# Sliding-window attention into a two-layer MLP: the order of the first loads and visits, and the form of the last output tile

## The chip, the core and the metric

The kernel runs on one core of a Trainium2 chip, in one launch. The metric is the device time of that core in microseconds (us); the time given for a kernel is the median of its runs. A core has TensorE (PE, matrix multiply, with its weight loads PEld), VectorE (DVE), ScalarE (ACT), GpSimd (POOL) and SyncE (SP). In this kernel POOL mostly issues DMAs that load and convert float32 to bfloat16, and SP issues the stores and the DMA transposes.

## The reference

Attention over 8 batches, 8 heads, 576 positions and head size 64, in which a position sees only those at most 32 away; its output, rearranged to 4608 tokens of 512, goes through a layer with an elementwise function between two matrix products.

```python
def _attn_ref(q, k, v) -> np.ndarray:
    B, H, S, D = q.shape
    window = 32
    scale = 1.0 / np.sqrt(D)
    scores = scale * np.matmul(q, k.transpose(0, 1, 3, 2))
    pos = np.arange(S)
    mask = np.abs(pos[:, None] - pos[None, :]) <= window
    scores = np.where(mask, scores, -1000000000.0)
    scores = scores - np.max(scores, axis=-1, keepdims=True)
    attn = np.exp(scores)
    attn = attn / (np.sum(attn, axis=-1, keepdims=True) + 1e-09)
    return np.matmul(attn, v).astype(np.float32)
...
def _moe_ref(x, w_in, w_out) -> np.ndarray:
    h = x @ w_in
    beta = 1.0
    neg = h <= -beta
    pos = h >= beta
    mid = ~neg & ~pos
    g = np.where(pos, h, np.where(neg, 0.0, (h + beta) ** 2 / (4.0 * beta)))
    _ = mid
    return (g @ w_out).astype(np.float32)
...
    x = np.ascontiguousarray(attn_out.transpose(0, 2, 1, 3)).reshape(B * S, H * D)
    return _moe_ref(x=x, **moe_kwargs)
```

Here x has 4608 rows of 512, w_in is 512 by 2048 and w_out 2048 by 512. The inputs are random; the output is float32.

## The kernel before

**Visits.** The second half of the problem sets the beat. The 4608 tokens are cut into 18 blocks of 256 (`TB`), the 2048 hidden columns into 8 groups of 256. The loop at L423 goes over visits a = 8 t + f: visit a multiplies the block t of x (kept transposed as `xT`, a ring of four batches' tokens) by the group f of w_in, eight matmuls of 256 columns into the PSUM tile `hp` (L444). ACT then computes `rr`, a rectified half of h + 1 (L448); DVE makes `mx`, the larger of h and `rr` (L450), and `gT`, the product of `rr` capped at 1 with `mx` (L451), which is the elementwise function. There are 144 visits and 8 turns of the loop without one.

**Quarters.** The second product runs in quarters. Quarter x (L405) is the quarter ff = x mod 4 of the hidden rows for the output tile tt = x div 4 of 128 tokens: four matmuls of 512 columns into the PSUM tile `op` (L414). After its fourth quarter a tile is copied to SBUF by ACT (L420) and stored by SP (L421). From visit 16 on, quarter a - 8 follows visit a; the first eight stand in a table (L364), as quarter needs the piece of `w_out` with its number ff and the `gT` of two visits. The last tile of all (`last`) is treated apart: it runs column quarter by column quarter, each with all 16 hidden groups (16 matmuls of 128 columns), a copy and a store of its own.

**Attention** is placed between the visits, by hand, in the table `ev` (L365 to L391): `scores` and `scores8` (L202, L229) multiply k by q and take the exponential on ACT; `sums` (L256) multiplies by v and by ones, and its end computes ln and exp on ACT (L290, L291) and leaves a DVE multiply into `xT` in the list `muls`, which `flush` (L302) issues later. `eng` tells how the band mask is put on: as matmuls on PE that add a bias ahead of the scores (`add_mask`, L195) when it is None, as a DVE multiply (L193) otherwise. The attention of batch b must be in `xT` before the blocks that hold its tokens are visited.

**Loads and transposes.** For the batches 0 to 2 (`LONG`), q and k come in two halves of four DMAs each (`load_long`, L80) and are transposed on PE (`tpose`, L169) through PSUM tiles of `ps_s` and `ps_n`, one buffer each, with a copy to SBUF by ACT or DVE; from batch 3 on SP's DMA transposes do it (`xpose`, L184). The lists of POOL's DMA issues are written out at L148 to L155 with `put` and `mix`; `load_w_in` (L104) loads a range of w_in's columns for one half h of the partitions, so a range needs two DMAs. POOL's issues run in their order; each one waits for the landing of the eighth before it, as eight semaphores are used in turn. `qjp` (L50) is a pool from which nothing is taken.

**The start.** Ahead of the loop (L328 to L356) the first half of batch 0 is transposed and goes through scores and sums, with matmuls on zeros in between (`keep_warm`, L314). The second half of batch 0 is transposed at visit 1 (L392: q at position 1, k at 1.5), its scores and sums are placed at visits 2 to 5 (L378 to L381), and visit 8 is the first that needs its tokens. PSUM: `ps_h` has two buffers for `hp`, `ps_o` two for `op` (visits 6 and 7 and `scores8` of batch 0 borrow them), `ps_s` and `ps_n` one pair of banks each.

Of the kernel before, what the change touches and what calls it, by code (L numbers as in the profile page):

```python
# [15 lines left out]
def kernel(  # L16
# [19 lines left out]
    nc = tc.nc  # L36
    B, H, S, D = q.shape
    NT, DM, DFF = out.shape[0], 512, 2048
# [3 lines left out]
    MAIN = 480  # L42
# [4 lines left out]

    const = ctx.enter_context(tc.tile_pool(name="const", bufs=1))
    nat = ctx.enter_context(tc.tile_pool(name="nat", bufs=2))
    qjp = ctx.enter_context(tc.tile_pool(name="qjp", bufs=2))  # L50
    ktp = ctx.enter_context(tc.tile_pool(name="ktp", bufs=3))
    ptp = ctx.enter_context(tc.tile_pool(name="ptp", bufs=2))
    smp = ctx.enter_context(tc.tile_pool(name="smp", bufs=2))
# [21 lines left out]
    V, P, A = nc.vector, nc.gpsimd, nc.scalar  # L75
# [65 lines left out]
    def halves(b, half):  # L141
        return [(load_long, b, half, t, y) for t in range(2) for y in range(NY)]

    def put(todo):
        for fn, *x in todo:
            fn(*x)

    w = [(load_w_in, c, c + d, h) for c, d in ((0, 256), (256, 256), (512, 512), (1024, 512), (1536, 512)) for h in range(2)]  # L148
    x = halves(0, 1)
    put(w[:4] + x[:4] + w[4:5] + x[4:] + w[5:])  # L150
    mix(halves(1, 0), [(load_w_out, 0)])
    put([(load_w_out, 1), (load_w_out, 2)] + [(load_v, 1, n) for n in range(4)])
    mix(halves(1, 1), [(load_w_out, 3)])
# [102 lines left out]
    def sums(b, y1, lo, hi, pool=ps_n):  # L256

        bb = two_banks(pool)
        w = hi - lo
        todo = []  # L260
        if lo < MAIN:
            ys, D0 = (y1,), w
            for par in range(2):
                a0 = max(lo, 32 * par)
                off = 32 - 64 * par
                todo.append((None, a0 - lo, hi - lo, lambda a, h, par=par, a0=a0, off=off: (
                    pt[b][HD[a], h, y1, par, a0 + off:hi + off])))
                for c2 in range(4):
                    q0, q1 = max(0, 128 * c2 - off, lo), min(128 * c2 + 128 - off, hi)
                    if q0 < q1:  # L270
                        todo.append((NC * y1 + 2 * c2 + par, q0 - lo, q1 - lo, lambda a, h, par=par, q0=q0, q1=q1, off=off: (
                            pt[b][HD[a], h, y1, par, q0 + off:q1 + off])))
        else:
            ys, D0 = (0, 1), 2 * w
            todo.append((None, 0, 2 * w, lambda a, h: pt8[b][HD[a], h].rearrange("p y j -> p (y j)")))
            for y in ys:
                todo.append((NC * y + 8, y * w, y * w + w, lambda a, h, y=y: pt8[b][HD[a], h, y]))
                for c in (None, NC * y + 7):
                    todo.append((c, y * w, y * w + 64, lambda a, h, y=y: pt[b][HD[a], h, y, 1, 448:512]))
        for n, (c, c0, c1, p) in enumerate(todo):  # L280
            o = D0 if c is None else 0
            for a in range(2):
                for h in range(2):
                    nc.tensor.matmul(bb[HD[h], a, o + c0:o + c1], ones[HD[a]] if c is None else vn[b][HD[a], c, h],  # L284
                                     p(a, h), start=n == 0, stop=True, skip_group_check=True)

        def end():
            lr = smp.tile([128, 2, 256], FP, name="lr", bufs=1)
            rc = smp.tile([128, 2, 256], FP, name="rc")
            A.activation(lr[:, :, :D0], bb[:, :, D0:2 * D0], AF.Ln)  # L290
            A.activation(rc[:, :, :D0], lr[:, :, :D0], AF.Exp, scale=-1.0)  # L291
            r0 = (b * S + lo) % RING
            o = xT.rearrange("p (a y) t -> p a y t", a=2)[:, :, ys[0]:ys[-1] + 1, r0:r0 + w]
            if len(ys) == 1:
                o = o[:, :, 0]
                muls.append(lambda: V.tensor_mul(o, bb[:, :, :D0], rc[:, :, :D0]))  # L296
            else:
                like = "p a (y j) -> p a y j"
                muls.append(lambda: V.tensor_mul(o, bb[:, :, :D0].rearrange(like, y=2), rc[:, :, :D0].rearrange(like, y=2)))  # L299
        return end  # L300

    def flush():  # L302
        while muls:
            muls.pop(0)()
# [56 lines left out]

    NB = NT // TB
    NF = DFF // 256
    quarters = {11: ([], [0]), 12: ([], [1]), 13: ([], [2]), 14: ([], [4, 5]), 15: ([6], [3, 7])}  # L364
    ev, tps = {}, {}  # L365

    def at(a, *todo):

        ev.setdefault(a, []).extend(x for x in todo if x)

    def steps(b, cut):

# [2 lines left out]
                yield (sums, b, y1, lo, hi), (scores, b, (y1, y1 + 1), (0, 2), (2 * k, 2 * k + 2))  # L375
        yield (sums, b, 0, MAIN, S), (scores8, b)

    at(2, (scores, 0, (0, 1), (0, 2), (2, 4)), (scores8, 0, ps_o))  # L378
    at(3, (sums, 0, 0, TB, MAIN), (scores, 0, (1, 2), (0, 2), (2, 4)))
    at(4, (sums, 0, 1, TB, MAIN, ps_s))  # L380
    at(5, (sums, 0, 0, MAIN, S))  # L381
    seq = [x for b in range(1, B) for x in steps(b, 224)]
    at(15, seq[0][0], (*seq[1][0], ps_s))
    for n, a in enumerate((20, 22, 23, 27)):
        at(a, seq[2 + n][0])
    for n, a in enumerate((11, 12, 19, 20, 22, 26, 27)):
        at(a, seq[n][1])
    sl = [30, 32, 35, 39, 42, 45, 49, 52, 56, 59, 62, 65, 69, 73, 77, 81, 84, 88, 92]
    sl += [96, 99, 103, 106, 110, 113, 116, 120, 124, 128]
    for n, a in enumerate(sl):  # L390
        at(a, seq[6 + n][0], seq[7 + n][1] if n < len(sl) - 1 else None)  # L391
    for b, half, *a in ((0, 1, 1, 1.5), (1, 0, 9, 10), (1, 1, 17, 18), (2, 0, 24, 25), (2, 1, 28, 29)):  # L392
        for t in range(2):
            tps[a[t]] = [(b, 2 * half + part, t) for part in range(2)]
    loads, xps = {}, {}
    for b in range(LONG, B):
        a = sl[5 * (b - 1) - 7] - 17
# [7 lines left out]
    def quarter(x):  # L405

        tt, ff = divmod(x, 4)
        if tt not in op:
            op[tt] = ps_o.tile([128, DM], FP, name="op", tag="op"), []
        o, done = op[tt]  # L410
        rows, last = slice(128 * tt, 128 * tt + 128), tt == NT // 128 - 1
        c = slice(128 * ff, 128 * ff + 128) if last else slice(0, DM)
        for j in range(2 * NF) if last else range(4 * ff, 4 * ff + 4):
            nc.tensor.matmul(o[:, c], gT[tt // 2][:, j, 128 * (tt % 2):128 * (tt % 2) + 128], w_out[:, j, c],  # L414
                             start=j == 0 if last else not done, stop=j == 2 * NF - 1 if last else len(done) == 2 * NF - 1,
                             skip_group_check=True)
            done.append(j)
        if last or len(done) == 2 * NF:
            osb = osp.tile([128, DM], FP, name="osb")
            A.copy(osb[:, c], o[:, c])  # L420
            nc.sync.dma_start(out=out[rows, c], in_=osb[:, c])  # L421

    for a in range(NF * NB + NF):  # L423
        t, f = divmod(a, NF)
        eng = None if a < 12 else V
        pre, post = quarters.get(a, ([], [a - NF] if a >= 2 * NF else []))
        for b, x in loads.get(a, []):
            if x < 2:
                load_nat(b, x)
            else:  # L430
                for n in range(4):
                    load_v(b, n)
        flush()
        if t < NB:
            if f == 0:
                gT[t] = gtp.tile([128, 2 * NF, TB], BF, name="gT", tag="gT")
            r0 = TB * t % RING
            if a in (6, 7):
                hp = ps_o.tile([128, 2, TB], FP, name="hp", tag="op")
            else:  # L440
                hp = ps_h.tile([128, 2, TB], FP, name="hp", tag="hp")
            for j in range(2):
                for n, kk in enumerate((0, 2, 1, 3)):
                    nc.tensor.matmul(hp[:, j], w_in[:, kk, 256 * f + 128 * j:256 * f + 128 * j + 128],  # L444
                                     xT[:, kk, r0:r0 + TB], start=n == 0, stop=n == 3)

            rr = ewp.tile([128, 2, TB], FP, name="rr")
            A.activation(rr, hp, AF.Relu, scale=0.5, bias=0.5)  # L448
            mx = ewp.tile([128, 2, TB], FP, name="mx")
            V.tensor_max(mx, hp, rr)  # L450
            V.scalar_tensor_tensor(gT[t][:, 2 * f:2 * f + 2], rr, 1.0, mx, op0=ALU.min, op1=ALU.mult)  # L451
        for x in pre:
            quarter(x)
        ends = []
        for fn, *x in ev.get(a, []):
            if fn is sums:
                ends.append(sums(*x))
            else:
                pool = (x.pop(),) if x[-1] in (ps_s, ps_n, ps_o) else ()
                fn(*x, eng, *pool)  # L460
        for end in ends:
            end()
        for x in post:
            quarter(x)
        for part in (a, a + 0.5):
            copies = [tpose(b, n, t, (A.copy, V.tensor_copy)[i if a > 15 else 0], tp1((ps_s, ps_n)[i]))
                      for i, (b, n, t) in enumerate(tps.get(part, []))]
            for x in copies:
                x()
        for x in xps.get(a, []):  # L470
            xpose(*x)

# [29 lines left out]
```

## Time and profile before

| What | Value |
|---|---|
| median of 3 runs | 324.28 us (324.18 to 324.35) |
| the profiled execution's own time | 324.18 us |
| its span, first to last instruction | 322.3 us |
| mean granted TensorE clock | 0.989 |
| PE: hp matmuls (L444) | 1152, 150.4 us busy |
| PE: op matmuls (L414) | 624, 147.2 us busy |
| DMA, over the span | 34.54 MB, mean 107 GB/s |
| DMA, busy share by 40 slices | full to slice 16, light from slice 24 |

The issues of the loads, from the profile's part on DMAs (median time from issue to landing): a w_in DMA of 128 KB takes 4.7 us, one of 256 KB 7.4; the small q and k pieces of 72 KB 5.3 and 4.9; a w_out piece of 512 KB 9.4; an output tile of 256 KB 2.4.

How to read it: PE, DVE and the others are busy for the sums of their instructions, which overlap; a matmul's duration includes its drain, so that successive ones overlap in the rows, and the distance from one start to the next is what PE pays. A wait is shown as idle time ahead of an instruction with what ended it. Times in the timeline count from the start of the span. The granted clock is the share of its full speed that TensorE was allowed.

### The profile page before, as it was taken

Reading aid. Unit: us, or ns where it says so; the run is one execution under the profiler, and the core shown is the slowest. Engines: PE = TensorE matmul, PEld = TensorE weight load, DVE = VectorE, ACT = ScalarE, POOL = GpSimd, SP = SyncE. Lnnn points to the kernel's source line nnn. Section 1 sums busy time; section 2 is a strip of 40 time slices with the busy share of each in tenths; the row PEclk is TensorE's granted clock in tenths of the full one; section 3 lists DMA queues with packets and bytes.
Section 4 is the critical chain, followed back from the end, with each engine's and each line's share of the span. In section 5 each row is a group of like instructions: output and inputs, shape, how many; then the busy total and the mean of one; then the engine's idle time right before and its main releaser. Section 6 shows DMA issues by size and latency. Waiting matters only on the chain.

```text
span 322.3 us, 8645 instructions
## 1 busy us (share of the span) xinstructions
PE 307.8 (96%) x3691; PEld 205.1 (64%) x3691; DVE 246.5 (76%) x384; ACT 194.9 (60%) x323; POOL 86.4 (27%) x120
## 2 busy tenths in 40 slices
PE   8959799999999999999999999999999999999994
PEld 3547655566666666666666666666666666666654
DVE  2335975887888888888888888888888888887750
ACT  3648765676776666765666666666576666654331
POOL 8973837698304503221411200000000000000000
PEclk9978999999999999999999999999999999999999
DMA  9999999999999999929991945005410000000102
GB/s 145 142 152 192 153 180 109 185 157 165 152 154 173 168 131 173 167 48 100 194 161 39 108 100 115 35 33 108 96 48 35 33 35 36 33 35 33 67 33 67
DMA packets 121462, 34.54 MB, mean 107 GB/s; under 512 B 108752, under 2 KB 116688, under 8 KB 121424
## 3 DMA queue, kind: packets, MB, share of 16 engines
q0 software_dynamic: 92128, 18.06, 71.9%
q1 hardware_dynamic: 29296, 15.93, 20.6%
q8 instruction: 29, 0.48, 0.6%
q14 instruction: 9, 0.07, 0.1%
HBM read 36.70 MB, written 9.44 MB: 143 GB/s over the span
## 4 chain that ended last, share of the span: by engine, by line
PE 83%; DVE 5%; ACT 3%; DMA 3%; POOL 3%; issue 2%; ACTq 0%; POOLq 0%
PE op L414 38%; PE hp L444 36%; PE bb L284 6%; PE bb L218 2%; DVE mx L450 2%; DMA kn<-in_k_dram 2%; DMA w_in<-in_moe_w_in_dram 1%; PE tp L179 1%; DVE gT L451 1%; POOL kn L85 1%; POOL vn L101 1%; DVE xT L296 1%; ACT lr L290 1%; ACT rc L291 1%; ACT pt L226 1%
## 5 line engine op out<-in xcount | busy, mean ns | idle before, releaser
L444 PE MATMUL hp<-xT,w_in 128*128 128x256 bf16 x1152 | 150.4, 274 | 3.0 <-DVE xT L299 1.3
L414 PE MATMUL op<-w_out,gT 128*128 128x512 bf16 (+1 forms) x624 | 147.2, 363 | 1.1 <-ACT osb L420 1.1
L444 PEld LDWEIGHTS <-w_in 128*128 128x128 bf16 x1152 | 112.2, 98 | 45.1 <-issue 3.7
L448 ACT ACTIVATE rr<-hp 128x512 f32<-128x512 f32 x144 | 85.5, 595 | 91.1 <-PE hp L444 87.7
L450 DVE TENSOR_TENSOR mx<-hp,rr 128x512 f32<-128x512 f32 x144 | 99.3, 690 | 42.4 <-ACT rr L448 40.2
L451 DVE SCALAR_TENSOR_TENSOR gT<-rr,mx 128x512 bf16<-128x512 f32 x144 | 99.6, 692 | 4.9
L414 PEld LDWEIGHTS <-gT 128*128 128x128 bf16 x624 | 55.5, 98 | 41.5 <-issue 1.5
L226 ACT ACTIVATE pt<-bb 128x1024 bf16<-128x1024 f32 (+1 forms) x33 | 33.1, 1010 | 6.0 <-PE bb L218 4.7
L101 POOL DMA_DIRECT2D vn<-in_v_dram x32 | 27.7, 886 | 30.6 <-PE bb L218 28.8
L296 DVE TENSOR_TENSOR xT<-bb,rc 128x512 bf16<-128x512 f32 (+1 forms) x32 | 21.1, 658 | 11.3 <-ACT rc L291 10.8
L420 ACT COPY osb<-op 128x512 f32<-128x512 f32 (+1 forms) x39 | 21.3, 549 | 12.6 <-PE op L414 12.2
L291 ACT ACTIVATE rc<-lr 128x512 f32<-128x512 f32 (+2 forms) x40 | 23.5, 587 | 1.3
L93 POOL DMA_DIRECT2D qn<-in_q_dram x10 | 12.3, 1245 | 40.9 <-DMA qT<-qn 40.9
L290 ACT ACTIVATE lr<-bb 128x512 f32<-128x512 f32 (+2 forms) x40 | 22.0, 550 | 1.4 <-PE bb L284 1.3
L193 DVE TENSOR_TENSOR pt<-pt,mask 128x1024 bf16<-128x1024 bf16 (+1 forms) x34 | 20.9, 616 | 0.2 <-ACT pt L226 0.2
L284 PE MATMUL bb<-pt,ones 64*64 64x256 bf16 (+3 forms) x352 | 19.5, 255 | 1.5 <-DVE xT L296 0.6
L284 PE MATMUL bb<-pt,vn 64*64 64x128 bf16 (+3 forms) x712 | 18.2, 204 | 0.0
L284 PEld LDWEIGHTS <-ones 64*64 64x64 bf16 x352 | 10.5, 105 | 10.4 <-issue 9.4
L284 PEld LDWEIGHTS <-vn 64*64 64x64 bf16 x712 | 16.7, 107 | 0.0
L85 POOL DMA_DIRECT2D kn<-in_k_dram x24 | 13.0, 554 | 10.5 <-issue 3.4
L218 PE MATMUL bb<-qT,kT 64*64 64x128 bf16 x520 | 13.4, 220 | 0.8 <-DVE kT L182 0.8
L85 POOL DMA_DIRECT2D qn<-in_q_dram x20 | 11.0, 571 | 7.8 <-DMA vn<-in_v_dram 3.1
(44 smaller groups left out, 100.2 us busy)
## 6 DMA issues: line engine op xcount, KB each, us to landing
out_dram<-osb SPq DMA_DIRECT2D x35, 256.0 KB, 2.4
vn<-in_v_dram POOLq DMA_DIRECT2D x32, 144.0 KB, 5.5
qn<-in_q_dram POOLq DMA_DIRECT2D x10, 288.0 KB, 7.0
kn<-in_k_dram POOLq DMA_DIRECT2D x10, 288.0 KB, 8.5
w_out<-in_moe_w_out_dram POOLq DMA_DIRECT2D x4, 512.0 KB, 9.4
kn<-in_k_dram POOLq DMA_DIRECT2D x24, 72.0 KB, 4.9
w_in<-in_moe_w_in_dram POOLq DMA_DIRECT2D x6, 256.0 KB, 7.4
qn<-in_q_dram POOLq DMA_DIRECT2D x20, 72.0 KB, 5.3
```

What stands on the lines that cost most here:

```text
L85: (eng or nc.gpsimd).dma_start(out=dst[b, half][32 * y:32 * y + 32], in_=src[b].rearrange("(h y) s d -> y h (s d)", h=2)[y] .rearrange("h ...
L101: nc.gpsimd.dma_start(out=vn[b][64 * a:64 * a + 64, :, h], in_=v[b, y:y + 2].rearrange("y s d -> (y s) d") .rearrange("(c r) d -> r c d", ...
L226: A.activation(p, ps[:, :, :128 * n].rearrange(like, y=m), AF.Exp, scale=D ** -0.5)
L284: nc.tensor.matmul(bb[HD[h], a, o + c0:o + c1], ones[HD[a]] if c is None else vn[b][HD[a], c, h], p(a, h), start=n == 0, stop=True, skip_g ...
L290: A.activation(lr[:, :, :D0], bb[:, :, D0:2 * D0], AF.Ln)
L291: A.activation(rc[:, :, :D0], lr[:, :, :D0], AF.Exp, scale=-1.0)
L296: muls.append(lambda: V.tensor_mul(o, bb[:, :, :D0], rc[:, :, :D0]))
L414: nc.tensor.matmul(o[:, c], gT[tt // 2][:, j, 128 * (tt % 2):128 * (tt % 2) + 128], w_out[:, j, c], start=j == 0 if last else not done, st ...
L444: nc.tensor.matmul(hp[:, j], w_in[:, kk, 256 * f + 128 * j:256 * f + 128 * j + 128], xT[:, kk, r0:r0 + TB], start=n == 0, stop=n == 3)
L448: A.activation(rr, hp, AF.Relu, scale=0.5, bias=0.5)
L450: V.tensor_max(mx, hp, rr)
L451: V.scalar_tensor_tensor(gT[t][:, 2 * f:2 * f + 2], rr, 1.0, mx, op0=ALU.min, op1=ALU.mult)
```

## The change

Four things differ.

1. **Loads.** Before, POOL issued w_in columns 0 to 512 (four DMAs), the second half of batch 0's q, one half of w_in columns 512 to 1024, the second half of k, and the rest of w_in. After, q and k follow each other behind the first 512 columns, and the columns 512 to 1024 come in two ranges of 256 (four DMAs in place of two).
2. **Early visits.** The transposes of batch 0's second half become entries of `ev`, with four `keep_warm` matmuls behind those of q, and the second of each pair of copies goes to DVE at visit 1. At visit 3 the scores stand ahead of the sums, and the PSUM pairs are assigned anew at visits 3 to 5. In visits 1 to 5 the DVE multiplies into `xT` are issued behind the visit's own `mx` and `gT` and no longer ahead of its matmuls. The scores of batch 1 at visits 11 and 12 move behind the quarters of these visits (11.5, 12.5), both with the mask on PE; the transposes of batches 1 and 2 move to half positions (9.5, 10.5 and so on).
3. **Quarters.** The first eight stand behind visits 9 (quarter 0), 11 (4), 12 (1), 13 (5, 2), 14 (6) and 15 (3, 7). Before: 11 (0), 12 (1), 13 (2), 14 (4, 5), 15 (6 ahead of the attention, then 3, 7).
4. **The last tile.** The treatment by column quarters is gone: tile 35 takes its four quarters like all others, one copy of 512 columns and one store.

Removed besides: the pool `qjp`.

```diff
-    qjp = ctx.enter_context(tc.tile_pool(name="qjp", bufs=2))
...
-    w = [(load_w_in, c, c + d, h) for c, d in ((0, 256), (256, 256), (512, 512), (1024, 512), (1536, 512)) for h in range(2)]
-    x = halves(0, 1)
-    put(w[:4] + x[:4] + w[4:5] + x[4:] + w[5:])
+    w = [(load_w_in, c, c + d, h) for c, d in ((0, 256), (256, 256), (512, 256), (768, 256), (1024, 512), (1536, 512))
+         for h in range(2)]
+    put(w[:4] + halves(0, 1) + w[4:])
...
-    quarters = {11: ([], [0]), 12: ([], [1]), 13: ([], [2]), 14: ([], [4, 5]), 15: ([6], [3, 7])}
-    ev, tps = {}, {}
+    quarters = [(9, 0), (11, 4), (12, 1), (13, 5), (13, 2), (14, 6), (15, 3), (15, 7)]
+    ev = {}
...
+    def through(b, half, t):
+        return [(tpose, b, 2 * half + part, t, part) for part in range(2)]
...
+    at(1, *through(0, 1, 0), (keep_warm, 4, ps_o, "op"))
+    at(1.5, *through(0, 1, 1))
     at(2, (scores, 0, (0, 1), (0, 2), (2, 4)), (scores8, 0, ps_o))
-    at(3, (sums, 0, 0, TB, MAIN), (scores, 0, (1, 2), (0, 2), (2, 4)))
-    at(4, (sums, 0, 1, TB, MAIN, ps_s))
-    at(5, (sums, 0, 0, MAIN, S))
+    at(3, (scores, 0, (1, 2), (0, 2), (2, 4), ps_n), (sums, 0, 0, TB, MAIN, ps_s))
+    at(4, (sums, 0, 1, TB, MAIN))
+    at(5, (sums, 0, 0, MAIN, S, ps_s))
...
-    for n, a in enumerate((11, 12, 19, 20, 22, 26, 27)):
+    for n, a in enumerate((11.5, 12.5, 19, 20, 22, 26, 27)):
         at(a, seq[n][1])
...
-    for b, half, *a in ((0, 1, 1, 1.5), (1, 0, 9, 10), (1, 1, 17, 18), (2, 0, 24, 25), (2, 1, 28, 29)):
+    for b, half, *a in ((1, 0, 9.5, 10.5), (1, 1, 17.5, 18.5), (2, 0, 24.5, 25.5), (2, 1, 28.5, 29.5)):
         for t in range(2):
-            tps[a[t]] = [(b, 2 * half + part, t) for part in range(2)]
+            at(a[t], *through(b, half, t))
...
-        rows, last = slice(128 * tt, 128 * tt + 128), tt == NT // 128 - 1
-        c = slice(128 * ff, 128 * ff + 128) if last else slice(0, DM)
-        for j in range(2 * NF) if last else range(4 * ff, 4 * ff + 4):
-            nc.tensor.matmul(o[:, c], gT[tt // 2][:, j, 128 * (tt % 2):128 * (tt % 2) + 128], w_out[:, j, c],
-                             start=j == 0 if last else not done, stop=j == 2 * NF - 1 if last else len(done) == 2 * NF - 1,
-                             skip_group_check=True)
+        for j in range(4 * ff, 4 * ff + 4):
+            nc.tensor.matmul(o, gT[tt // 2][:, j, 128 * (tt % 2):128 * (tt % 2) + 128], w_out[:, j],
+                             start=not done, stop=len(done) == 2 * NF - 1, skip_group_check=True)
             done.append(j)
-        if last or len(done) == 2 * NF:
+        if len(done) == 2 * NF:
             osb = osp.tile([128, DM], FP, name="osb")
-            A.copy(osb[:, c], o[:, c])
-            nc.sync.dma_start(out=out[rows, c], in_=osb[:, c])
+            A.copy(osb, o)
+            nc.sync.dma_start(out=out[128 * tt:128 * tt + 128, :], in_=osb)
+
+    def run(pos):
+        todo = []
+        for fn, *x in ev.get(pos, []):
+            if fn is sums:
+                todo.append(sums(*x))
+            elif fn is tpose:
+                part = x.pop()
+                todo.append(tpose(*x, (A.copy, V.tensor_copy)[part if pos < 2 or pos > 16 else 0], tp1((ps_s, ps_n)[part])))
+                if part:
+                    while todo:
+                        todo.pop(0)()
+            elif fn is keep_warm:
+                keep_warm(*x)
+            else:
+                pool = (x.pop(),) if x[-1] in (ps_s, ps_n, ps_o) else ()
+                fn(*x, eng, *pool)
+        for end in todo:
+            end()
 
     for a in range(NF * NB + NF):
         t, f = divmod(a, NF)
-        eng = None if a < 12 else V
-        pre, post = quarters.get(a, ([], [a - NF] if a >= 2 * NF else []))
+        eng = None if a < 14 else V
+        post = [x for n, x in quarters if n == a] if a < 2 * NF else [a - NF]
...
-        flush()
+        if a == 0 or a > 5:
+            flush()
...
-        for x in pre:
-            quarter(x)
-        ends = []
...
-        for end in ends:
-            end()
+        flush()
+        run(a)
         for x in post:
             quarter(x)
-        for part in (a, a + 0.5):
-            copies = [tpose(b, n, t, (A.copy, V.tensor_copy)[i if a > 15 else 0], tp1((ps_s, ps_n)[i]))
-                      for i, (b, n, t) in enumerate(tps.get(part, []))]
-            for x in copies:
-                x()
+        run(a + 0.5)
```

More of the change, by code (lines that the diff above doesn't have):

```diff
@@ L432 @@
                     load_v(b, n)
-        flush()
+        if a == 0 or a > 5:
+            flush()
         if t < NB:
-            if f == 0:
+            if t not in gT:
                 gT[t] = gtp.tile([128, 2 * NF, TB], BF, name="gT", tag="gT")
@@ L451 @@
             V.scalar_tensor_tensor(gT[t][:, 2 * f:2 * f + 2], rr, 1.0, mx, op0=ALU.min, op1=ALU.mult)
-        for x in pre:
-            quarter(x)
-        ends = []
[L455 to L460, printed above, removed]
-        for end in ends:
-            end()
+        flush()
+        run(a)
         for x in post:
             quarter(x)
-        for part in (a, a + 0.5):
-            copies = [tpose(b, n, t, (A.copy, V.tensor_copy)[i if a > 15 else 0], tp1((ps_s, ps_n)[i]))
-                      for i, (b, n, t) in enumerate(tps.get(part, []))]
-            for x in copies:
-                x()
+        run(a + 0.5)
         for x in xps.get(a, []):
```

## The prediction

> **What bounds the kernel now.** I read the page first. TensorE (PE) is busy 96% of the span, so a change must remove PE idle time, slow PE time, or the end.
>
> ```profile
> PE 307.8 (96%) x3691; PEld 205.1 (64%) x3691; DVE 246.5 (76%) x384; ACT 194.9 (60%) x323; POOL 86.4 (27%) x120
> ...
> PE 83%; DVE 5%; ACT 3%; DMA 3%; POOL 3%; issue 2%; ACTq 0%; POOLq 0%
> ```
>
> Then PE's timeline of the start (columns: start, duration, what; in brackets the idle time before it). Visit 1 ends at 17.2, the q transposes run, and PE stands 3.65 us for the second half of k. Visits 2 and 3 and the scores run slowly; visit 8 waits 1.31 us for xT.
>
> ```profile
> 15.53 1.69 PE L444 MATMUL hp<-xT,w_in 128*128 128x256 bf16 x14 [0.23 <-DVE xT L296]
> 17.26 0.69 PE L179 MATMUL tp<-ident,qn 128*64 128x128 bf16 x18
> 21.61 1.17 PE L179 MATMUL tp<-ident,kn 128*64 128x128 bf16 x18 [3.65 <-DMA kn<-in_k_dram]
> 22.85 1.87 PE L444 MATMUL hp<-xT,w_in 128*128 128x256 bf16 x8
> ...
> 28.25 1.05 PE L444 MATMUL hp<-xT,w_in 128*128 128x256 bf16 x8
> ...
> 34.79 1.91 PE L444 MATMUL hp<-xT,w_in 128*128 128x256 bf16 x16 [1.31 <-DVE xT L299]
> ```
>
> The windows view of PE (length, busy, granted clock, DMA share, GB/s) explains the slowness: after a stretch with 1.49 us busy the clock is half for two stretches; a stretch with 2.11 busy did not lower it.
>
> ```profile
> 16.42:19.83 3.41, 1.49 (x26) 1.00 1.05 149
> 19.83:23.25 3.42, 1.57 (x21) 0.50 1.12 157
> 23.25:26.66 3.41, 3.41 (x43) 0.50 1.14 162
> ...
> 33.48:36.90 3.42, 2.11 (x26) 1.00 1.06 147
> ```
>
> Last the timeline of the end: a quarter-tile copy, PE waiting for it, 16 narrow matmuls, and again.
>
> ```profile
> 314.11 0.58 ACT L420 COPY osb<-op 128x512 f32<-128x512 f32 x1 [2.87 <-PE op L414]
> 314.72 5.26 SPq L421 DMA_DIRECT2D out_dram<-osb  x5
> 315.00 0.27 ACT L420 COPY osb<-op 128x128 f32<-128x128 f32 x1 [0.31 <-PE op L414]
> 315.32 1.05 PE L414 MATMUL op<-w_out,gT 128*128 128x128 bf16 x16 [0.35 <-ACT osb L420]
> ...
> 319.35 0.27 ACT L420 COPY osb<-op 128x128 f32<-128x128 f32 x1 [1.19 <-PE op L414]
> ```
>
> **The end.** Column quarters go. A group of eight 512-column matmuls (row at 47.10) takes 1.89, a group of four 1.03: 0.216 for each and a drain of 0.17. PE begins its last run at 309.59 with 20 of them, so the last tile's 16 run from 313.92 to 317.38 and are out at 317.55. The copy is 0.58 (row 314.11), so 318.15. The single 256 KB store replaces four of 64 KB: the stores issued at 304.32 and 311.26 landed in 2.0 us, so 320.2. Before, the last quarter copy ended at 319.62 and its store, issued at 319.64, landed 1.6 later, at 321.2. Gain **1.0**. Other bound of the store: the one issued at 297.37 took 3.8, a loss of 0.8.
>
> **Loads.** POOL issues the second k half straight behind q, and w_in columns 512 to 1024 behind it in four pieces. Issue by issue: four k at 0.54 (waiting, as now, for slots: 14.70 to 16.50), four pieces of 0.62 to 19.0, four old ones to 21.5; the last old one ended at 21.50 already, so nothing behind on POOL starts later. The queues moved 149 to 162 GB/s from 16.4 to 26.7. By the DMA view (issue plus time to landing) q lands at 17.1 as now; 288 KB of k at 152 GB/s are there at 19.0 (now 16.49 + 5.0 = 21.5). The set k plus w_in to 1024 is the one that was complete at 17.01 + 5.7 = 22.7; its first 256 KB of w_in come at 21.0. Columns 1024 to 1536 have the same bytes ahead and land at 26.4 as now, so do w_out and v of batch 1 (quarter 3's piece: 37.16 + 11.7 = 48.9).
>
> **Visits 1 to 8.** q transposes to 17.95, four keep-warm matmuls (0.216 each) to 18.8, the first k part from 19.0. The second q copy moves from ACT to DVE, where it stands behind gT of visit 1 (19.07 + 0.69) until 20.4; the second k part waits for its PSUM, runs 20.45 to 20.8 and is copied by 21.6. Visit 2 has its weights at 21.0 and ends at 21.9 (8 in 0.87 at full clock), scores and the tail scores take 1.1, visit 3 runs 23.0 to 23.9, scores and sums end at 25.2. Then PE waits for the weights of visit 4 until 26.4 (now 28.25). From there: hp out at 27.44, rr to 28.04, mx and gT to 29.4 (0.73 + 0.61), and only then the multiply of the first sums, since the early flush now stands behind the elementwise pair; queued behind it are the last sums, which take that PSUM pair: 30.05 to 30.5. Their ln, exp (0.5 each, 30.6 to 31.6), then on DVE the other multiply until 31.95 and theirs to 32.5. Visit 8 starts at **32.5 instead of 34.79**. Bounds for the weights of visit 4: 25.2, when all earlier work ends (at the 196 GB/s that the row from 26.37 to 29.04 shows they would be there), a further 1.2 gained; and 0.8 lost if the four small pieces come like the first four, in the 4.87 us from 10.81 (v's landing) to 15.68, against 4.1 for the two large ones now (2.87 after q, 1.25 after k). While PE waits there, the second sums, visit 5 and the last sums stand behind it, and the DVE multiplies wait for those.
>
> [...]
>
> **The clock.** Up to 19.83 PE is now busy 1.49 + 0.86 (keep-warm) + 0.4 (k part) = 2.75, over the 2.11 that kept the clock. Before 26.66 it is 23.25 to 25.2 plus visit 4's first part, 2.0 to 2.2: at that row, so I take full speed. The other end, 1.49, gives a half-speed spell whose price is the chain's PE part, visit 4 (0.87) and the last sums (0.4): 1.3.
>
> [...] If the clock falls at 19.83, the work from 20.45 takes 7.2 us (1.87 + 1.32 and so on, from the slow rows), visit 4 starts 1.3 late, and the sum is 321.9.
>
> **Visits 8 to 16.** From 34.79 to the end of visit 15's sums (51.51) PE has 16.0 of work and 0.72 of wait (visit 10 for mx). Quarter 0 now stands ahead of visit 10 and fills that wait. Added: the second scores of batch 1 masked on PE, 0.81 (row at 40.61) against 0.35 (43.26), +0.46; DVE loses its 0.61 there, off the path. Quarter 6 only changes places. Sums end at 32.5 + 16.46 = 48.96; their ln, exp and multiply take 2.8 as now (51.51 to 54.31), covered by quarters 3 and 7 (1.73) and idle. Visit 16's gated matmuls start at 51.8 instead of 54.31: **2.55**. What each quarter needs is there: w_out pieces at 38.6, 41.9 and 48.9 for quarters 1, 2 and 3 at 41.0, 44.5 and 49.0, v at 46.3 for the sums at 48.0. Quarter 3 has 0.1 to spare; up to 0.7 more lies in the idle time now before visit 16 (0.69).
>
> **Carried to the end.** After 54.31 no PE gap is over 0.64 and each is ended by ACT or DVE. The DMA transposes of batch 3 land at 93.29 + 9.8 = 103.1, their scores start at 108.6, then at 106.0: still covered. The unused pool costs nothing: no instruction names it.
>
> Sum: 2.55 + 1.0 = 3.55. The span 322.3 becomes 318.75; around it lie 1.9, so 324.18 becomes 320.63. The profiled run is 0.1 under the median of 324.28; I forecast **320.6**.
>
> **Rivals.** (A) The gain is kept, 320.6: chance 0.68; its own range is 319.4 to 321.7.
> (B) The clock falls once, before visit 4 or at 19.83: 321.9; two stretches that nothing covers, 1.7 each, 324.0. For: visit 4's wait. Against: 2.11 kept it. 0.10.
> (C) w_in hides the earlier k: visit 4's weights land 2.3 later, at 28.7, and visit 8 stands where it was; left are 0.26 (0.72 - 0.46) and 1.0: 322.9. For: the DMAs are full until 50. Against: the bytes ahead are equal. 0.10.
> (D) Slower: the queue paces by piece, not by byte. If each of the four small pieces takes 2.30, the interval of the 256 KB piece that landed at 25.0, they need 9.2 instead of 4.1; 5.1 late less 3.55 is 325.7. It is slower than before from 1.91 a piece on. For: one of the first four took 1.87. Against: others took 0.50 and 0.76, and q pieces 0.36. 0.07.
> (E) DMAs faster, visit 4 unhindered: 319.4 or less. 0.05.
>
> A measurement of this kernel tells 0.2% (0.65 us) from no change. Faster: A, E, and nearly all of B and C, 0.88; same 0.04 (the far ends of B and C); slower 0.08 (D, and B with a third half-speed stretch, 325.7). The range reaches down to E with a store that lands in 1.6, as the small ones did, 319.0, and up to C, 322.9, which takes in the clock's price and a store of 3.8 (322.4).
>
> **What would show it.** Right: no wait over 0.7 for kn; clock 1.00 from 19.8 to 26.7; a wait of about 1.2 for w_in at visit 4; visit 8 near 32.5, visit 16 near 51.8; one 0.58 copy last and a store of 2.0. Wrong: kn landing after 20, a half clock anywhere after 6.2, visit 16 after 53, a PE wait at quarters 1, 2 or 3 for w_out.

## The result and the profile after

| | before | after |
|---|---|---|
| median of the runs | 324.31 us (324.18 to 325.73) | 321.20 us (321.01 to 321.45) |
| ratio, 95% interval | | 0.9895 (0.9866 to 0.9923) |
| profiled execution, its span | 324.18, 322.3 | 321.09, 319.3 |
| granted clock over the span | 0.989 | 0.998 |
| visit 4, visit 8, visit 17 start | 28.25, 34.79, 55.83 | 27.32, 33.35, 53.66 |
| visit 143 starts; last store landed | 308.72; 321.2 | 306.56; 318.0 |

The kernel became 3.1 us faster, against a forecast of 3.7. All of it lies ahead of visit 17 and behind visit 143: every visit from 17 to 143 starts 2.16 earlier. Of these, 1.44 are won ahead of visit 8 and the rest, some 0.7, between visits 8 and 17.

PE's timeline of the start, after (columns as in the prediction; the row from 31.44 holds visits 6 to 9, and visit 8 starts in it at 33.35):

```profile
17.98 1.04 PE L317 MATMUL z<-warm 128*128 128x512 bf16 x4
20.45 0.69 PE L178 MATMUL tp<-ident,kn 128*64 128x128 bf16 x18 [1.44 <-DMA kn<-in_k_dram]
21.80 1.03 PE L466 MATMUL hp<-xT,w_in 128*128 128x256 bf16 x8 [0.66 <-DMA w_in<-in_moe_w_in_dram]
...
27.32 1.03 PE L466 MATMUL hp<-xT,w_in 128*128 128x256 bf16 x8 [1.80 <-DMA w_in<-in_moe_w_in_dram]
...
31.02 0.28 PE L283 MATMUL bb<-pt,ones 64*64 64x192 bf16 x4 [1.01 <-DVE xT L295]
...
31.44 3.81 PE L466 MATMUL hp<-xT,w_in 128*128 128x256 bf16 x32
...
49.91 1.89 PE L417 MATMUL op<-w_out,gT 128*128 128x512 bf16 x8 [0.54 <-DMA w_out<-in_moe_w_out_dram]
51.63 1.33 PE L466 MATMUL hp<-xT,w_in 128*128 128x256 bf16 x8
```

The one wait of 3.65 us has become a series: 1.44 for k, 0.66 for visit 2's weights, 1.80 for visit 4's, 1.01 for a multiply into xT, 0.54 for the last piece of w_out. Visits 2 and 3 now take 1.03 and 1.05, where visit 2 took 1.87. The windows view shows why. Its stretches of 3.41 us are counted back from 318.01, where the clock fell behind the last matmuls of this run (the last section has the lengths between the clock's changes):

```profile
17.63:21.05 3.42, 1.98 (x37) 1.00 1.04 121
21.05:24.46 3.41, 2.75 (x52) 1.00 1.18 140
24.46:27.87 3.41, 1.61 (x55) 1.00 1.16 183
```

The clock stayed at 1.00 in all three and behind them, though the last has no more than 1.61 us of work. The end, after:

```profile
307.43 7.93 PE L417 MATMUL op<-w_out,gT 128*128 128x512 bf16 x36
...
309.11 7.24 SPq L423 DMA_DIRECT2D out_dram<-osb  x3
...
315.40 0.59 ACT L422 COPY osb<-op 128x512 f32<-128x512 f32 x1 [2.87 <-PE op L417]
```

PE runs through without a wait, one copy follows, and the last of the three stores lands 2.0 after its issue at 316.0.

### The profile page after: what moved, and what is told of

Same layout as the page of the kernel before. It is cut to its first block, busy times and chain, and to the rows that moved or that the text cites. A ratio compares the mean times of both kernels' runs of the same rounds, so it can differ in the third digit from the quotient of the medians.

```text
span 319.3 us, 8552 instructions
## 1 busy us (share of the span) xinstructions
PE 305.3 (96%) x3651; PEld 201.6 (63%) x3651; DVE 247.1 (77%) x385; ACT 193.6 (61%) x318; POOL 87.7 (27%) x122
## 4 chain that ended last, share of the span: by engine, by line
PE 84%; DMA 4%; POOL 4%; DVE 4%; ACT 3%; issue 1%; POOLq 0%; ACTq 0%
PE op L417 38%; PE hp L466 37%; PE bb L283 5%; DMA w_in<-in_moe_w_in_dram 4%; PE bb L217 2%; POOL kn L84 1%; PE tp L178 1%; DVE gT L473 1%; DVE mx L472 1%; POOL vn L100 1%; POOL w_in L104 1%; ACT rr L470 1%; ACT lr L289 1%; DVE xT L295 1%; ACT rc L290 1%
## 5 line engine op out<-in xcount | busy, mean ns | idle before, releaser
L417 PE MATMUL op<-w_out,gT 128*128 128x512 bf16 x576 | 146.6, 380 | 0.5 <-DMA w_out<-in_moe_w_out_dram 0.5
L417 PEld LDWEIGHTS <-gT 128*128 128x128 bf16 x576 | 53.5, 98 | 42.1 <-issue 0.5
L100 POOL DMA_DIRECT2D vn<-in_v_dram x32 | 27.7, 882 | 26.9 <-PE bb L217 26.3
L422 ACT COPY osb<-op 128x512 f32<-128x512 f32 x36 | 20.9, 582 | 11.5 <-PE op L417 11.1
L92 POOL DMA_DIRECT2D qn<-in_q_dram x10 | 12.3, 1237 | 40.0 <-DMA qT<-qn 39.7
L192 DVE TENSOR_TENSOR pt<-pt,mask 128x1024 bf16<-128x1024 bf16 (+1 forms) x33 | 20.3, 614 | 0.2 <-ACT pt L225 0.2
L84 POOL DMA_DIRECT2D kn<-in_k_dram x24 | 13.0, 549 | 10.3 <-DMA w_out<-in_moe_w_out_dram 3.8
L92 POOL DMA_DIRECT2D kn<-in_k_dram x10 | 12.1, 1215 | 5.4 <-DMA kT<-kn 3.3
```

The costliest lines, as they stand in the source:

```text
L92: nc.gpsimd.dma_start(out=x[:, :, h], in_=src[b, NY * h:NY * h + NY].rearrange("y s d -> (y s) d") .rearrange("(u p) d -> p u d", p=128))
L100: nc.gpsimd.dma_start(out=vn[b][64 * a:64 * a + 64, :, h], in_=v[b, y:y + 2].rearrange("y s d -> (y s) d") .rearrange("(c r) d -> r c d", ...
L417: nc.tensor.matmul(o, gT[tt // 2][:, j, 128 * (tt % 2):128 * (tt % 2) + 128], w_out[:, j], start=not done, stop=len(done) == 2 * NF - 1, s ...
```

## The experiments

The experiments are edits of two shortened kernels, the yardsticks, which leave out the DMA transposes: q and k of batches 3 to 7 are not transposed, and their scores take those of the batch three places earlier. All other work stays. Medians are of 6 to 12 runs; the ratio is to the full kernel before, run beside them on the same chip. The experiments ran in three groups, on three chips, and beside them the kernel before had medians of 324.31, 324.45 and 324.76; both yardsticks are of the first group. With this and the spread of the runs, medians less than some 0.7 us apart (12 runs each) or 1 us (six) are not told apart.

```diff
     def xpose(b, t):
 
-        nc.sync.dma_start_transpose(out=qkT(b, t).rearrange("d (u p) -> d u p", p=128),
-                                    in_=(qn, kn)[t][b].rearrange("p u h d -> p (u h d)"))
+        kT[b] = kT[b - 3]
```

**The yardsticks.**

> The kernel before without its ten DMA transposes of batches 3 to 7, whose scores take q and k of the batch three places earlier; all matmuls, activations and loads stay. It is the yardstick for the kernels that are compared here. PE bounds the stretch in which the transposes ran and their consumers came 5.5 us after them: 324.2, visits 0 to 17 where they were, to 0.1. If the transposes cost anything: some tenths less.

> The changed kernel without the DMA transposes in the same way: 321.1, visits 17 to 143 some 2.2 earlier than in the shortened kernel before. If the transposes had eaten part of the gain: a larger distance than 3.1 between the two shortened kernels.

Measured: 324.49, ratio 1.0002 (0.9983 to 1.0022), and 321.51, ratio 0.9906 (0.9876 to 0.9935). The distance is 3.0, so the transposes are no part of the gain.

**The last tile alone.**

```diff
-        rows, last = slice(128 * tt, 128 * tt + 128), tt == NT // 128 - 1
...
-        if last or len(done) == 2 * NF:
+        if len(done) == 2 * NF:
             osb = osp.tile([128, DM], FP, name="osb")
-            A.copy(osb[:, c], o[:, c])
-            nc.sync.dma_start(out=out[rows, c], in_=osb[:, c])
+            A.copy(osb, o)
+            nc.sync.dma_start(out=out[128 * tt:128 * tt + 128, :], in_=osb)
```

> The shortened kernel before with only the last tile changed: four ordinary quarters, one 512-column copy, one 256 KB store. If the two gains simply add: 1.0 us less than the shortened kernel before (323.2), visit 143 where it was, last copy ending near 318.15. If the store of 256 KB lands late (3.8 us) or the end is set by something else: 324.2 or more.

Measured: 323.58, ratio 0.9976 (0.9952 to 0.9999), 0.9 under its yardstick. From visit 143 to the landing of the last store are 11.5 us, as in the changed kernel, and 12.5 before. The end is worth 1.0, by itself.

**Keep-warm matmuls alone.** Order of loads and all else as before.

```diff
             for x in copies:
                 x()
+            if part == 1:
+                keep_warm(16, ps_o, "op")
```

> The shortened kernel before with 16 keep-warm matmuls of 512 columns (3.5 us) behind the q transposes of visit 1, so that PE is not idle while k is awaited. Clock theory (most of what is won before visit 8 is that visits 2 and 3 run at full clock, since the weights of visit 4 land at the same time in both orders): clock 1.00 throughout, visit 4 near 27.0 instead of 28.25, visit 8 near 33.5 instead of 34.8, about 1.2 us faster (323.0). Load theory (the earlier k is what counts): visit 8 less than 0.3 earlier, 324.0 to 324.2.

Measured: 323.43, ratio 0.9965 (0.9947 to 0.9982), 1.1 under the yardstick. PE's timeline of this kernel:

```profile
18.15 3.63 PE L317 MATMUL z<-warm 128*128 128x512 bf16 x16
21.83 0.69 PE L179 MATMUL tp<-ident,kn 128*64 128x128 bf16 x18
23.38 1.03 PE L443 MATMUL hp<-xT,w_in 128*128 128x256 bf16 x8 [0.86 <-DMA w_in<-in_moe_w_in_dram]
...
27.08 1.05 PE L443 MATMUL hp<-xT,w_in 128*128 128x256 bf16 x8
```

Visit 2 is no earlier than in the yardstick (22.87) and k no sooner there, yet visit 4 starts at 27.08 instead of 29.07: work on zeros, with which the clock stayed at 1.000 in this run, where the yardstick's profile has 0.51 and 0.50 from 21.57 to 28.40, won what the clock theory said. At visit 8 1.35 of it is left (34.27 against 35.62). Eleven of its twelve runs have a clock of 0.997 or more; none of the yardstick's twelve has (0.987 to 0.995).

**The new loads alone, and with keep-warm matmuls** (the list of loads of the change in the kernel before; the second adds 8 keep-warm matmuls at the place above).

> The shortened kernel before with nothing but the new list of loads (k behind q, w_in to 1024 in four pieces). Load theory: k's transposes near 19.5, visit 2 near 21.5, and most of the early gain is there: visit 8 near 33.5, 323.0 or less. Clock theory: PE is busy less than half of the stretch around 17 to 21, the clock falls as before, visits 2 and 3 at half speed still end by 25.5 to 27, visit 4 starts at 27 to 28 and the time is 323.5 to 324.3.

> The shortened kernel before with the new list of loads and 8 keep-warm matmuls behind the q transposes: the fourth corner beside the shortened kernel before (324.5), the one with keep-warm matmuls alone (323.4) and the one with the new loads alone (323.05). Clock theory (the new loads help because PE waits less and the clock falls less): the two do not add; clock 1.00 in nearly all runs, 322.3 to 322.8, most of it from the runs that no longer have a half-speed stretch. If loads and clock were two independent gains: 324.5 - 1.1 - 1.4 = 322.0 or less.

Measured: 323.05, ratio 0.9946 (0.9927 to 0.9965), and 323.31, ratio 0.9956 (0.9934 to 0.9977). Alone, the keep-warm matmuls gave 1.1 and the loads 1.4; together 1.2. They don't add, as the clock theory has it, in which both act on the same loss. A common bound behind both, such as the landings below, would look the same; this pair of runs does not tell them apart. And the theory's number, 322.3 to 322.8, was missed: six of the twelve runs kept a clock of 0.997 or more (median 322.7), the other six did not (0.992 to 0.995, median 323.7). The profiled one lost it after visit 4's wait of 2.39 for w_in: 1.29 us of work from 25.75 to 29.17, then a clock of 0.51 to 32.58. The idle time had gone one place on. In the run with the loads alone visit 8 was already at 33.18, near the expected 33.5; there a wait of 1.12 for the last piece of w_out took part of it back.

**The changed kernel without its four keep-warm matmuls.**

```diff
-    at(1, *through(0, 1, 0), (keep_warm, 4, ps_o, "op"))
+    at(1, *through(0, 1, 0))
```

> The shortened changed kernel without its four keep-warm matmuls at visit 1. Clock theory: with 0.86 us less, PE is busy some 1.6 us of 3.4 around the wait for k, between the 1.49 that lowered the clock and the 2.11 that did not; if it falls, visits 2 and 3 run at half speed, visit 4 is 0.5 to 1.3 later than in the shortened changed kernel (26.7) and the median 0.5 to 1.3 above its 321.5. Load theory: the same time whatever the clock, as visit 4 waits 1.4 to 1.8 us for w_in anyway.

Measured: 320.91, ratio 0.9889 (0.9870 to 0.9908): not slower than its yardstick. The windows view of its profiled run:

```profile
18.75:22.16 3.41, 1.42 (x23) 1.00 1.10 140
22.16:25.58 3.42, 3.42 (x44) 0.50 1.08 156
```

The clock fell, as expected, and visit 4 was 0.4 later in this run (27.06 against 26.67), but the weights of visit 4 landed at 26.9 and set that. Here the load theory holds at visit 4: one stretch of 3.4 us at half speed is hidden by w_in. It is not hidden in full: visit 8 comes 6.40 after visit 4, where it came 6.03 after it in the yardstick, as PE waits 1.54 and not 1.16 for the multiply into xT. These four matmuls are worth nothing that six runs can show.

**w_in's columns 512 to 1024 in two pieces, not four.**

```diff
-((0, 256), (256, 256), (512, 256), (768, 256), (1024, 512), (1536, 512))
+((0, 256), (256, 256), (512, 512), (1024, 512), (1536, 512))
```

> The shortened changed kernel with w_in's columns 512 to 1024 in two DMAs of 256 KB, behind q and k, in place of four of 128 KB. If the queue moves bytes, whatever the piece: the weights of visit 4 land at 26.4 to 27.2 as before, visit 2 starts 0.8 to 1.3 later (its range is now complete only at 22.4 to 22.7), and since visit 4 waits for w_in anyway, visit 8 and the time stay to 0.4 (321.1 to 321.9). [...] If visit 2 sets the pace: 322.3.

Measured: 323.59, ratio 0.9967 (0.9949 to 0.9984), 2.1 over its yardstick: the outcome in which visit 2 sets the pace, and over it. PE's timeline, then the windows view:

```profile
23.47 1.87 PE L465 MATMUL hp<-xT,w_in 128*128 128x256 bf16 x8 [2.80 <-DMA w_in<-in_moe_w_in_dram]
...
26.58 1.89 PE L465 MATMUL hp<-xT,w_in 128*128 128x256 bf16 x8
...
29.88 1.05 PE L465 MATMUL hp<-xT,w_in 128*128 128x256 bf16 x8
```

```profile
19.25:22.66 3.41, 0.77 (x18) 1.00 1.11 162
22.66:26.07 3.41, 2.60 (x28) 0.50 1.16 183
26.07:29.49 3.42, 3.42 (x60) 0.50 1.21 195
```

Visit 2 needs both pieces whole (the second landed at 23.3), so it waits 2.80 us; PE has 0.77 us of work in a stretch of 3.41, the clock is 0.50 for the two behind it, and visit 4 starts at 29.88 though its weights had landed at 26.3. With k early and w_in late, the loss is the old one with another name on the wait. I had priced the later visit 2 as hidden and left out what its wait does to the clock.

**Multiplies into xT ahead of every visit.**

```diff
-        if a == 0 or a > 5:
-            flush()
+        flush()
```

> The shortened changed kernel with the multiplies into xT issued ahead of every visit, as before the change, and not behind mx and gT in visits 1 to 5. The wait of 1.0 to 1.2 us of PE for the multiply at visit 5 goes (0.3 or less), visit 8 starts 0.6 to 0.9 earlier. If the start is bound by that chain of multiplies: visit 17 as much earlier, 320.8. If it is bound by landings: PE waits more for the last piece of w_out ahead of quarter 3 (now 0.5 to 0.6, then 1.1 to 1.5), visit 17 gains 0.3 or less, 321.2 to 321.5.

Measured: 320.71, ratio 0.9887 (0.9864 to 0.9910). PE's timeline:

```profile
27.20 1.03 PE L464 MATMUL hp<-xT,w_in 128*128 128x256 bf16 x8 [2.34 <-DMA w_in<-in_moe_w_in_dram]
...
32.69 1.58 PE L464 MATMUL hp<-xT,w_in 128*128 128x256 bf16 x13 [0.68 <-DVE xT L297]
...
49.90 1.89 PE L416 MATMUL op<-w_out,gT 128*128 128x512 bf16 x7 [1.17 <-DMA w_out<-in_moe_w_out_dram]
```

The wait at visit 5 (1.16 in the yardstick) is gone, and visit 8 comes 5.49 after visit 4 instead of 6.03. But the wait ahead of quarter 3 is 1.17 instead of 0.61 and ends with the landing; visit 17 is at 53.36, not earlier than the yardstick's 53.01. In the profiled runs the landing theory holds. The median is 0.8 lower; its runs (319.9 to 321.6) overlap with the yardstick's (320.1 to 322.2), and four of six against two of six have the full clock, so I don't credit the edit with it.

**The first quarters behind the visits of before.**

```diff
-    quarters = [(9, 0), (11, 4), (12, 1), (13, 5), (13, 2), (14, 6), (15, 3), (15, 7)]
+    quarters = [(11, 0), (12, 1), (13, 2), (14, 4), (14, 5), (15, 6), (15, 3), (15, 7)]
```

> The shortened changed kernel with its first eight quarters behind the visits where they stood before (11, 12, 13, 14, 14, 15, 15, 15). Prediction's step: quarter 0 ahead of visit 10 fills a wait of 0.72 for mx; without it that wait is back, and quarter 6 behind visit 15 adds to what follows the sums: visit 17 0.5 to 0.9 later, 322.1. If the last piece of w_out sets visit 16 in any case: 0.2 or less.

Quarter 6 is not quite where it was: it stands behind the attention of visit 15, where it stood ahead of it.

Measured: 321.21, ratio 0.9890 (0.9856 to 0.9925): no loss that the runs can show. PE's timeline:

```profile
37.99 1.03 PE L465 MATMUL hp<-xT,w_in 128*128 128x256 bf16 x8 [0.72 <-DVE mx L471]
...
50.56 2.76 PE L416 MATMUL op<-w_out,gT 128*128 128x512 bf16 x12
```

The wait of 0.72 is back. But quarter 6 no longer delays the sums, which end a quarter's 0.86 sooner for it and pay for the wait; it runs while their ln, exp and multiply are awaited. From visit 8 to visit 17 this run takes 20.17, the yardstick 20.31, and the shortened kernel before, with the wait and with quarter 6 ahead of the sums, 21.04. So this is another order of the same worth, and does not show that the new one is worth nothing. There is no wait for the last piece of w_out, which landed at 50.0, ahead of the row from 50.56; but this run came to visit 8 at 34.74, the yardstick at 32.70.

**More keep-warm matmuls, and everything together.** The first has 8 at visit 1 and 5 behind visit 3; the second adds the early multiplies and a last tile copied in halves:

```diff
+            if tt == NT // 128 - 1:
+                for i, copy in enumerate((A.copy, V.tensor_copy)):
+                    half = osp.tile([128, DM // 2], FP, name=f"osh{i}", bufs=1)
+                    copy(half, o[:, 256 * i:256 * i + 256])
+                    nc.sync.dma_start(out=out[128 * tt:128 * tt + 128, 256 * i:256 * i + 256], in_=half)
+                return
```

> The shortened changed kernel with 8 keep-warm matmuls at visit 1 in place of 4 and 5 more behind visit 3, where PE waits for w_in. Clock theory: its runs (320.1 to 322.2, clock 0.994 to 1.000) spread because some have a half-speed stretch; with PE busy all of them have 1.00 and lie at 320 to 321.2, median 320.7. If the spread comes from the landings alone: median 321.2 to 321.8, same spread, whatever the clock.

> The shortened changed kernel with three edits: the added keep-warm matmuls, the multiplies into xT ahead of every visit, and the last tile copied in two halves by ACT and DVE at once, each with a store of 128 KB. Sum of the parts: clock 1.00 in all runs, visit 8 near 32.5, visit 17 near 53.2 (bound by the last piece of w_out at 49.3 to 49.9), the copies 0.35 in place of 0.59 and a store of 1.8 in place of 2.0: 320.0 to 320.4. If DVE's copy from the same PSUM tile waits for ACT's: no gain at the end, 320.6.

Measured: 321.13, ratio 0.9892 (0.9862 to 0.9922), and 321.34, ratio 0.9892 (0.9865 to 0.9919). Five of six runs of the first have the full clock, but they reach from 320.65 to 322.00, so something besides the clock spreads them; that it is the landings was not shown. The second missed its 320.0 to 320.4. Its end:

```profile
315.18 0.37 ACT L424 COPY osh<-op 128x256 f32<-128x256 f32 x1 [2.87 <-PE op L417]
...
315.59 0.42 DVE L424 COPY osh<-op 128x256 f32<-128x256 f32 x1 [6.08 <-ACT osh L424]
```

DVE's half copy began when ACT's was done, so the two together take longer than the one copy of 0.59. No kernel tried here is clearly faster than the changed one.

## Why the prediction was right, and where it was off

**The end: right.** Forecast 1.0; from visit 143 to the last landing the time fell from 12.49 to 11.46. The single store landed in 2.0, the copy took 0.59. Behind that landing the span had 1.3 us where it had 1.1 before, which took 0.2 of it away.

**Loads: the mis-sized term.** k's last piece landed at 20.3, not 19.0, visit 2's second one at 21.7, not 21.0, and visit 4's at 27.2, not 26.4. The forecast moved k at 152 GB/s (the rate of the kernel before from 17.12 to 19.99) and let visit 4's weights stand still, as if only bytes counted. The windows view of one stretch, in the changed kernel and in the one with two large pieces:

```profile
17.20:23.00 5.80, 3.59 (x53) 1.00 1.14 131
17.20:23.00 5.80, 2.48 (x40) 0.97 1.07 149
```

In the nine profiled runs with the four small pieces the queues moved 126 to 136 GB/s there, in the five with two large ones 149 to 170. Visit 4's weights landed at 26.5 to 27.8 (median 27.25) in the nine, at 25.3 to 26.9 (26.35) in the five. The 0.8 by which visit 8 missed its 32.5 (33.35) is the 0.8 by which these weights missed theirs, a bound that stood in the prediction as the dear end, for small pieces. The spread is wide: the shortened changed kernel, with the same list, had the three landings at 19.2, 21.4 and 26.5, the earliest of the nine at visit 4.

**Visits 1 to 8: right in shape.** Visit 4 waits for w_in, the last sums for the multiply behind gT (31.02 against 30.05), visit 8 follows. All steps are later by the same 0.9. Visit 8 gained 1.44, not 2.29.

**Visits 8 to 17: right about the wait, wrong about the mask.** Quarter 0 did fill the wait of 0.72. The 0.46 charged for the second mask on PE did not come on top. These are the scores that were read as masked before, and the first scores after:

```profile
40.61 0.41 PE L198 MATMUL bb<-bias,ident 64*64 64x512 bf16 x4
41.07 0.42 PE L218 MATMUL bb<-qT,kT 64*64 64x128 bf16 x16
...
40.16 0.41 PE L197 MATMUL bb<-bias,ident 64*64 64x512 bf16 x4
40.41 0.39 PE L217 MATMUL bb<-qT,kT 64*64 64x128 bf16 x16
```

Before, the score matmuls began 0.46 after the mask, since their weight loads waited 0.35 for kT; after, they began 0.25 behind it. So a masked score takes 0.57 and not 0.81, the second mask costs 0.22 over the 0.35 without it, and the first score gives 0.24 back. The wait of 0.54 for w_out ahead of quarter 3 cost nothing: it lies, as the prediction allowed, within the 2.8 that ln, exp and multiply take from the end of the sums (49.37) to the gated matmuls of visit 16 (52.15). The stretch from visit 8 to 17 became 0.73 shorter, not 0.26. It takes 21.04 in the kernel before and its yardstick, 20.31 in the changed kernel and its yardstick, and 20.31 or 20.32 in four of the six edits of the latter; the others are the old quarters (20.17) and the early multiplies alone (20.67, with their wait of 1.17 for w_out). So two misses of opposite sign, 0.85 and 0.47, left a gain of 2.16 where 2.55 was forecast; that they cancel in part is luck.

**The clock: right, with luck.** The forecast laid the stretches where they lay in the profile before. In the profile after they lay 1.2 later, and the stretch ahead of visit 4 had 1.61 us of work, not 2.0 to 2.2, little above the 1.49 after which the clock fell in the profile before. All four timed runs kept it (0.998 to 1.000). But four of the six runs of the shortened changed kernel had 0.994 or 0.995 and a median of 321.8, against 320.7 for the two others: rival B, as a matter of the single run.

**Signs and rivals.** Two of the signs named for being wrong came: kn landed after 20, with a wait of 1.44, and PE waited at quarter 3 for w_out. Neither cost time of its own: visit 4 waited for w_in in any case, and the wait at quarter 3 is the covered one. The 0.2% (0.65 us) that a measurement was said to tell from no change was too sharp: the interval came out 0.3% (0.9 us) to either side. C (visit 8 where it was) is refuted by 33.35 against 34.79, but its ground, the full DMA queues (a share of 1.04 to 1.18 from 17.63 to 27.87), set the limit. D is refuted in its size: the four small pieces landed 0.7, 0.7 and 0.9 apart, not 2.3. What the forecast left out of the small pieces is their rate, 131 GB/s from 17.2 to 23.0 against 149 with two pieces of 256 KB. These land visit 4's weights sooner (26.35 against 27.25, the medians above) and still cost 2.1 us more than four of 128 KB, because the first user has to wait for whole pieces (2.80 us), and the clock falls in that wait (0.50 from 22.66 to 29.49).

What stays open: how the 1.44 ahead of visit 8 divide between the loads and the clock. The clock alone gave 1.1, the loads alone 1.4, both 1.2. That the new places of the early visits' work win anything there is not shown: with the loads alone visit 8 started at 33.18, between the 33.35 of the changed kernel and the 32.70 of its yardstick. The rest closes: 323.05 for the loads alone, less 0.9 for the end, less 0.73 for visits 8 to 17, is 321.4, and the whole measured 321.51. The 0.73 is read from rows; no run has the new quarters alone, and none the early part with the old end.

## What to carry to other kernels

When a load gates the first work, look past the wait itself at what the idle time does to the clock of the work behind it: here the wait of 3.65 us in the kernel before and that of 2.80 with two large pieces were each followed by 6.8 us at half the clock, those of 2.01 and 0.87 without the four keep-warm matmuls by 3.4. Cut a load so that the first user's share lands by itself, and price both sides: here the small pieces moved 131 GB/s where the large ones moved 149, for 5.8 us, and landed the later weights 0.9 later, and still won 2.1. Filling one wait moved it to the next landing here (with the early multiplies the wait of 1.16 at visit 5 went, and that of 0.61 ahead of quarter 3 became 1.17), so price an edit against the landing that comes after it.

## What the runs showed of the hardware

**The granted clock beside PE's work, in stretches of 3.41 us.** In the trace of the kernel before, full speed is on record from 6.18 to 19.83, half from 19.83 to 26.66; in that of the changed kernel, full from 3.98 to 318.01. The lengths of 13.65, 6.83 and 314.03 are 4, 2 and 92 times 3.413. In the windows views laid on such stretches, one at full speed was followed by half speed after 0.44 us of PE work (yardstick of the kernel before), 0.77 (two large pieces), 1.24 (new loads alone), 1.29 (new loads with keep-warm matmuls), 1.42 (without the four keep-warm matmuls), 1.47 (old quarters) and 1.49 (kernel before). It was followed by full speed after 1.61, 1.98 and 2.75 (changed kernel) and after 2.11 (kernel before). At half speed, 1.57 (kernel before), 2.42 (its yardstick) and 2.60 (two large pieces) were followed by another such stretch; 2.75 (new loads alone) and 3.41 (kernel before) were not. The falls whose end the views show lasted one such stretch or two. Between 1.49 and 1.61, and between 2.60 and 2.75, they have nothing. The nearest pair, from the kernel with the old quarters and, above, from the changed one (1.61):

```profile
24.44:27.85 3.41, 1.47 (x54) 1.00 1.22 196
27.85:31.27 3.42, 3.42 (x42) 0.50 1.24 206
```

The stretch from 17.63 above held 1.98 us of work, 1.04 of them without the transposes, and the clock stayed at 1.00, while it was 0.50 after the 1.47 of the old quarters, in which there is no transpose. By these two, the transposes' time counted here.

**Where the stretches lie differs from run to run**: the fall came at 19.83 in the kernel before and at 21.57 in its yardstick, which has the same start. The runs of the kernel before, 64 of them beside the experiments, fall into two groups: 24 with a clock of 0.995, which one stretch at half speed makes over the span (0.5 x 3.41 of 322.3 lost), have a median of 323.5; 40 with 0.987 to 0.989, near what two make, 324.8. So the second half-speed stretch goes with 1.2 us in this kernel, and the tight first runs (324.18 to 324.35) show less than its real spread.

**The smaller pieces moved fewer bytes in the same time.** From 17.2 to 23.0 the changed kernel moved 0.76 MB in 1342 packets (131 GB/s), the kernel before, whose w_in pieces landing there are of 256 KB, 0.89 MB in 937 (154 GB/s).
